# Three loads of x ahead of a store, an add on another engine, and a third float16 first stage in a Fourier-transform kernel

## The chip, the cores and the metric

The kernel runs on one core of a Trainium2 chip. The core has a matrix engine (TensorE, PE in the profile; its weight loads are PEld), three engines for elementwise work (VectorE is DVE, ScalarE is ACT, GpSimd is POOL) and SyncE (SP), which in this kernel issues every transfer. The metric is the device time of one execution in microseconds. The kernel before took 1434.9 us (median of 3 runs, 1434.13 to 1436.1).

## The reference

```python
X = np.fft.rfft(x, axis=1)                  # x is 8 x 3136 x 256, float32
y = np.fft.irfft(X * F[None], n=3136, axis=1)   # F = filt_r + 1j * filt_i
mixed = np.real(np.fft.fft(np.fft.fft(y, axis=1), axis=2))
u = y + mixed
un = (u - mean(u)) / np.sqrt(var(u) + 1e-06)    # over the last axis
out = u + np.maximum(un @ w_ch1, 0.0) @ w_ch2   # w_ch1 256 x 1024, w_ch2 1024 x 256
```

## The kernel before

**What is computed where.** Each of the 8 batches passes through a Fourier transform along the sequence, written as matrix products with tables: `forward1` is the first stage (14 steps of 112 x 512), `forward2` the second stage, the multiplication with the filter and the first stage back, `inverse2` the last stage back, whose results (y, halved into even and odd rows by `store`) go to `dy` in DRAM. Batch 0 works with float32 tables and has a first path of its own: the rows of the first group are formed directly from the tile `near` by the matmuls of L845, without `dy`. What is between the stages goes through DRAM: `bt` to `d_f` (L767, L754 and L760 for `near`), then `d_f` to the pieces `b` (L821).

The second half of the work is cut into 49 groups of 512 rows. For each, y is fetched from `dy` (L968), `prepare` adds the mixed part (matmuls L982, adds L992 on DVE), takes the moments (L1040, L1041), forms the four scales `sb` (L1046 to L1056), the normalised rows `un` (L1151, ACT), their two float16 halves `u` (L1154 on ACT, L1155 on POOL), and transposes them by DMA into `ut` (L1156, on SP). The first group is transposed by PE (L327, `utt`). Then `first_product` (L1181, 6 matmuls for each of 8 slices, followed by L1191 on ACT and L1192 on DVE) and `second_product` (L1211) do the two matrix products of the group. They are most of PE's work. The weights come from float64 words which ACT and DVE widen (L1231 to L1238) and split in halves (L1299, L1312: `w2s` is what L1211 loads).

**The first stage in two forms.** Batches named in `PLAIN`, 1 and 2, multiply x as float32 by a float32 table; the others scale x, split it into float16 halves on ACT and DVE and multiply three times. The step of `forward1`, cut:

```python
            if b in PLAIN:
                nc.tensor.matmul(p, table, x, start=True, stop=True)          # L530
                nc.scalar.activation(st[:, :, 0], p, AF.Copy, scale=sx[:112, 1:2])       # L532
                nc.vector.scalar_tensor_tensor(st[:, :, 1], p, sx[:112, 1:2], st[:, :, 0], ...)  # L533
                ...
            nc.scalar.activation(x16[:, 0], x, AF.Copy, scale=sx[:112, 1:2])  # L538
            nc.vector.scalar_tensor_tensor(x16[:, 1], x, sx[:112, 1:2], x16[:, 0], ...)  # L539
            for i, (hs, hx) in enumerate(((0, 0), (0, 1), (1, 0))):
                nc.tensor.matmul(p, s1[:, hs], x16[:, hx], start=i == 0, stop=i == 2)   # L544
```

L546 and L547 then split the result of the second form. The scale `sx` comes from the squares of x (L480 for batch 1, ahead of need; L319 for others), through a broadcast by PE (L312, `pb_x`).

**What sets the order.** The program calls these pieces from one loop over the slices; `todo`, a list of numbers and functions, says at which step weights and x are loaded and widened. A tile scheduler then puts the instructions of each engine in one order from its own timeline, and each engine runs its order strictly, waiting where an instruction's operands aren't there. `after(...)` forbids that something is put ahead of a named instruction (`"bt", 6`: the last `bt`; `"near"`; `"warm"`: small matmuls on still data, L294, whose results nobody reads; `"utt"`; `"turn"`). SP issues all transfers from one order too, and a transfer waits for the one eight before it.

## Time and profile before

| | |
|---|---|
| median of 3 runs | 1434.9 us (1434.13 to 1436.1) |
| the profiled execution's own time | 1433.79 us |
| its span, first to last instruction | 1432.0 us |
| granted TensorE clock, mean of the span | 0.994 |
| busy: PE, DVE, ACT, POOL | 1387.5, 1042.7, 756.3, 506.7 us |
| instructions | 29958 |

The profiled execution lies 1.1 us under the median. PE is busy 97% of the span; busy shares of the other engines are means over stages with different limits. A wait row says which engine waited at which line and operand for which engine's result; a timeline row gives the start, the length, the engine, the line and the shapes, and in brackets the idle time just before it with what ended it.

### The profile page before, as it was taken

The page shows a single profiled execution, that of the slowest core. Times are in us where ns is not written, and L with a number is a line of the kernel's source. Part 1 is how long each engine was busy: PE and PEld are TensorE (multiplying, and loading weights), DVE is VectorE, ACT ScalarE, POOL GpSimd, SP SyncE. Part 2 cuts the span into 40 slices and gives each one's busy share as a digit, 9 for nine tenths or more (in the row PEclk, how much of TensorE's full clock was granted, in tenths as well). Part 3 has the DMA queues.
Part 4 walks back from the last instruction along what each step waited for, and adds up shares of the span by engine and source line. Part 5 has one row for each costly group of instructions (what it writes and reads, how often), then busy time and mean ns, then how long its engine had stood idle before and what let it go on. Part 6 is the DMA issues. An engine that isn't in the chain of part 4 may idle for free.

```text
span 1432.0 us, 29958 instructions
## 1 busy us (share of the span) xinstructions
PE 1387.5 (97%) x11242; PEld 946.6 (66%) x11242; DVE 1042.7 (73%) x2317; ACT 756.3 (53%) x1421; POOL 506.7 (35%) x643
## 2 busy tenths in 40 slices
PE   8869899999999999999999999999999999999998
PEld 7736576567666776667766676666766667666666
DVE  7867684788698777877588867978779876555553
ACT  6775555546465544746546554655546464434341
POOL 2501681078103930167300960047401762011010
PEclk9989999999999999999999999999999999999999
DMA  9585987699857967579766987589585977452220
GB/s 349 189 272 172 263 201 243 192 224 228 258 155 193 246 160 244 169 204 232 169 224 190 239 193 223 150 242 228 128 272 164 227 177 192 117 154 80 82 59 30
DMA packets 434350, 276.98 MB, mean 193 GB/s; under 512 B 218877, under 2 KB 400845, under 8 KB 434205
## 3 DMA queue, kind: packets, MB, share of 16 engines
q1 hardware_dynamic: 434076, 275.02, 70.0%
q8 instruction: 88, 1.44, 0.4%
q14 instruction: 58, 0.47, 0.1%
q10 hardware_dynamic: 128, 0.05, 0.0%
HBM read 124.87 MB, written 99.17 MB: 156 GB/s over the span
## 4 chain that ended last, share of the span: by engine, by line
PE 70%; DMA 11%; DVE 7%; issue 4%; ACT 3%; POOL 3%; SPq 2%; DVEq 0%; ACTq 0%; POOLq 0%
PE h L1181 27%; PE acc L1211 27%; PE y L880 3%; DMA x<-x 3%; PE s L544 2%; PE mix L982 2%; PE s L530 2%; DMA y<-dy 1%; DMA at<-d 1%; PE i L739 1%; DVE y L992 1%; PE i L741 1%; PE i L740 1%; PE s L640 1%; DVE h L1192 1%
## 5 line engine op out<-in xcount | busy, mean ns | idle before, releaser
L1211 PE MATMUL acc<-w2s,h 128*128 128x256 f16 x4704 | 596.4, 273 | 3.7 <-ACT w2s L1312 2.6
L1181 PE MATMUL h<-ut,home 128*128 128x512 f16 x2352 | 582.0, 380 | 12.4 <-DVE h L1192 7.5
L1211 PEld LDWEIGHTS <-h 128*128 128x128 f16 x4704 | 455.1, 98 | 148.2 <-issue 13.9
L1191 ACT ACTIVATE h<-h 128x512 f16<-128x512 f32 x392 | 232.7, 595 | 375.6 <-PE h L1181 370.1
L1192 DVE SCALAR_TENSOR_TENSOR h<-h,h 128x512 f16<-128x512 f32 x392 | 267.7, 685 | 211.3 <-ACT h L1191 209.4
L1181 PEld LDWEIGHTS <-home 128*128 128x128 f16 x2352 | 221.7, 98 | 223.2 <-issue 33.9
L1155 POOL TENSOR_TENSOR u<-un,u 128x512 f16<-128x512 f32 x96 | 110.4, 1166 | 620.8 <-ACT u L1154 572.3
L992 DVE SCALAR_TENSOR_TENSOR y<-mix,alpha,y 128x508 f32<-128x508 f32 (+1 forms) x360 | 152.9, 476 | 3.9 <-DMA y<-dy 2.0
L657 POOL TENSOR_TENSOR yt<-yt,t 128x224 f32<-128x224 f32 x108 | 73.0, 676 | 130.4 <-DVE t L649 80.7
L1151 ACT ACTIVATE un<-y,sb 128x256 f32<-128x256 f32 x192 | 100.0, 590 | 34.0 <-DVE sb L1056 26.8
L1220 DVE SCALAR_TENSOR_TENSOR y<-acc,beta,y 128x512 f32<-128x512 f32 x98 | 71.3, 744 | 30.3 <-PE acc L1211 30.2
L743 DVE TENSOR_TENSOR bt<-i,bt 112x512 f16<-112x512 f32 x98 | 66.2, 684 | 33.0 <-ACT bt L742 31.2
L687 POOL TENSOR_TENSOR ef<-yt 128x224 f32<-128x224 f32 x112 | 72.2, 663 | 48.7 <-DVE sb L1052 34.8
L889 ACT ACTIVATE ys<-y,alpha 128x512 f32<-128x512 f32 x98 | 64.3, 684 | 40.8 <-PE y L880 40.4
L671 POOL TENSOR_TENSOR home<-yt,home 128x448 f16<-128x448 f32 x77 | 79.3, 1035 | 13.7 <-ACT home L670 13.7
L742 ACT CAST bt<-i 112x512 f16<-112x512 f32 x98 | 56.7, 584 | 45.4 <-PE i L741 41.5
L645 DVE SCALAR_TENSOR_TENSOR yt<-s,pF,ft 128x448 f32<-128x448 f32 x98 | 65.9, 676 | 17.1 <-PE s L641 16.2
L658 POOL TENSOR_TENSOR yt<-yt,t 128x224 f32<-128x224 f32 x108 | 74.6, 693 | 0.6 <-DVE yt L651 0.6
L1040 DVE BATCH_NORM_STATS2 st<-y 128x6 f32<-128x256 f32 x196 | 73.0, 411 | 0.2
L319 DVE TENSOR_REDUCE mx<-x 112x1 f32<-112x1024 f32 x42 | 51.0, 1214 | 23.8 <-DMA x<-x 23.4
L649 DVE SCALAR_TENSOR_TENSOR t<-s,pF,ft 128x448 f32<-128x448 f32 x98 | 66.1, 675 | 0.0
L717 POOL TENSOR_TENSOR eo<-ef,eo 128x448 f16<-128x448 f32 (+6 forms) x55 | 51.5, 940 | 29.3 <-ACT eo L716 27.9
(180 smaller groups left out, 1648.1 us busy)
## 6 DMA issues: line engine op xcount, KB each, us to landing
x<-x SPq DMA_DIRECT2D x55, 512.0 KB
out<-y SPq DMA_DIRECT2D x98, 256.0 KB
at<-d SPq DMA_DIRECT2D x49, 512.0 KB
b<-d SPq DMA_DIRECT2D x49, 512.0 KB
dy<-ys SPq DMA_DIRECT2D x206, 112.0 KB
y<-dy SPq DMA_DIRECT2D x90, 256.0 KB
d<-ast SPq DMA_DIRECT2D x98, 224.0 KB
d<-bt SPq DMA_DIRECT2D x98, 224.0 KB
```

The costliest lines, as they stand in the source:

```text
L657: nc.gpsimd.tensor_tensor(yh[:, 0], yh[:, 0], t2v[:, 1], op=ALU.subtract)
L658: marks["sum"] = nc.gpsimd.tensor_tensor(yh[:, 1], yh[:, 1], t2v[:, 0], op=ALU.add).ins
L671: nc.gpsimd.tensor_tensor(ylo, ytv, yhi, op=ALU.subtract)
L687: nc.gpsimd.tensor_tensor(ef[:, i], yt[:, 0, i], yt[:, 1, i], op=o)
L992: nc.vector.scalar_tensor_tensor(out, p, al, y, op0=ALU.mult, op1=ALU.add)
L1040: nc.vector.bn_stats(st[:m, 2 * t + k], y[:m, t, k])
L1151: nc.scalar.activation(un[:m, k], y[:m, t, k], AF.Identity, bias=sb[:m, i, 1:2], scale=sb[:m, i, 3:4])
L1155: marks["u16", g] = nc.gpsimd.tensor_tensor(u16[:m, :, :, 1], unv, u16[:m, :, :, 0], op=ALU.subtract).ins
L1181: marks["pe"] = nc.tensor.matmul(p[:, c0 : c0 + n].rearrange("p (t k q) -> p t k q", k=2, q=m), homes["w1s"][:, d, hw, 128 * f : 128 * f + ...
L1191: marks["relu"] = nc.scalar.activation(h[:, 0, :nt], p[:, :nt], AF.Relu).ins
L1192: marks["h"] = nc.vector.scalar_tensor_tensor(h[:, 1, :nt], p[:, :nt], 0.0, h[:, 0, :nt], op0=ALU.max, op1=ALU.subtract).ins
L1211: nc.tensor.matmul(acc[:m, k], h[:, hh, c0 : c0 + m], w2s[:, f, hw], start=f == 0 and k == 0 and i == 0, stop=f == 7 and k == 1 and i == 2,)
```

## The change

- `PLAIN` loses batch 2, so its first stage takes the form with halves.
- The first two pieces of batch 0 for `inverse2` are loaded by a new function, `load_piece`, at two numbers of `todo`, after the last `bt`; the mark `"piece"` stands for the last of them. Loads of the weights and the later loads of x now wait for `"piece"` in place of `("bt", 6)`, and x's pieces 5 and 6 for the first `y` piece.
- The first three loads of x move from 57 and 61.2 to 49.1 in `todo`; `take_words` from 56.9 to 49.
- The first pieces of `inverse2` (L903) come after `"turn"` and not after `"warm"`, and the six fillers behind each are gone; 20 fillers stand at one place instead, ahead of the transposes of group 0. `square_x` runs for pieces 0 to 2 together.
- The copy of two columns of `y` in the first group (L1086) moves from ACT to DVE.
- The calls of `give` and `fetch(1)` that stood before the loop move to its step 1, and `give` in the first steps runs at 0, 3 and 5 instead of 1 and 3.

```diff
-PLAIN = (1, 2)
+PLAIN = (1,)
...
-        with after(("bt", 6)):
+        with after("piece", ("y", 1) if q > 4 else ""):
             nc.sync.dma_start(sooner[q], a["x"][1, q])
...
+    pieces = {}
+
+    def load_piece(c):
+
+        bt = fp.tile([128, 4, 256], F32, tag="b2", name=f"b2_0_{c}", bufs=2)
+        with after(("bt", 6)):
+            marks["piece"] = nc.sync.dma_start(bt, blocks128(scratch[2][0], 4 * c, 4)).ins
+        pieces[c] = bt[:112]
+
...
-            if c < 7:
+            if c < 7 and not (b == 0 and c in pieces):
...
-        load(1 if b == 0 else 0)
+        if b:
+            load(0)
...
-                load(c // 2 + 1)
+                if b or c > 2:
+                    load(c // 2 + 1)
...
-            with after("warm" if c < 4 else "turn"):
+            with after("turn"):
                 marks["i2"] = nc.tensor.matmul(
...
-            if c < 4:
-                warm(6, "i2", p=idle[0])
...
-        nc.scalar.copy(y[row, t0, 1, 0:129:128], point[row, 0, 0:129:128])
+        nc.vector.tensor_copy(y[row, t0, 1, 0:129:128], point[row, 0, 0:129:128])
...
-        with after(("bt", 6)):
+        with after("piece"):
             nc.sync.dma_start(words[i], src.bitcast(I32).rearrange("p (n w) -> p n w", w=2))
...
-    todo += [(57, load_x, 0), (57, load_x, 1), (61.2, load_x, 2), (61.5, load_x, 3)]
+    todo += [(56.95, load_piece, 1), (56.96, load_piece, 2)]
+    todo += [(49.1, load_x, 0), (49.1, load_x, 1), (49.1, load_x, 2), (61.5, load_x, 3)]
...
-    todo += [(56.9, take_words, i) for i in (5, 6)]
+    todo += [(49, take_words, i) for i in (5, 6)]
...
-    for q in range(2):
+    for q in range(3):
         square_x(q)
...
-    square_x(2)
     next(first_group)
-    give(come[0] + 2)
+    warm(20, "i2", p=idle[0])
     for _ in first_group:
         pass
+    give(come[0] + 2)
...
-    give(need(511))
-    fetch(1)
...
-        if q in (1, 3) or q > 9:
+        if q in (0, 3, 5) or q > 9:
             give(min(come[0] + 1, soon(32 * q + SOON)))
+        if q == 1:
+            give(need(511))
+            fetch(1)
```

**SP, end of batch 0's first stage back.** Before, the transfers stand in this order, directly behind the loads of `near` (`x_0` to `x_4`: pieces of batch 1's x; `b_0_1`, `b_0_2`: the pieces for `inverse2`; `raw`: words of the weights; `dy`: the first store of y):

```order
L767 DMA d_f<-bt_6_0_763 112x512
L767 DMA d_f<-bt_6_1_772 112x512
L473 DMA x_0_838<-x 128x1024
L473 DMA x_1_840<-x 128x1024
L473 DMA x_2_922<-x 128x1024
L1255 DMA raw_836<-w 128x1024
L821 DMA b_0_1_920<-d_f 128x4x256
L1255 DMA raw_837<-w 128x1024
L473 DMA x_3_926<-x 128x1024
L821 DMA b_0_2_958<-d_f 128x4x256
L473 DMA x_4_1120<-x 128x1024
L826 DMA dy_919<-ys_2_960 28x4x256 x4
```

Now, with `x_0` and `x_1` just ahead of the first row shown (the new code's line 813 is `load_piece`, 1267 the weights):

```order
L473 DMA x_2_744<-x 128x1024
L767 DMA d_f<-bt_5_1_765 112x512
L754 DMA near_282<-d_f 96x1x512
L754 DMA near_283<-d_f 96x1x512
...
L767 DMA d_f<-bt_6_0_771 112x512
L767 DMA d_f<-bt_6_1_780 112x512
L813 DMA b_0_1_844<-d_f 128x4x256
L813 DMA b_0_2_846<-d_f 128x4x256
L1267 DMA raw_722<-w 128x1024
```

The three loads of x have moved ahead of the store of `bt_5_1` and of the loads of `near`; both pieces of `inverse2` have moved ahead of the weights.

**DVE, around the scales of group 2.** Before, the five steps of group 2's `sb` stand in this row, ahead of the adds of group 3's y (L992 of `y_1617`, which come six rows further on):

```order
L1052 RECIPROCAL sb_1535<-sb_1535 128x4
L1041 BN_AGGR mv_1723<-st_1724 128x2
L1053 SCALAR_TENSOR_TENSOR sb_1535<-sb_1535 128x4
L645 SCALAR_TENSOR_TENSOR yt_0_1671<-s_1_0_0_1672,pF,ft 128x448
L649 SCALAR_TENSOR_TENSOR t_1_0_0_1690<-s_1_0_0_1672,pF,ft 128x448
L1054 SCALAR_TENSOR_TENSOR sb_1535<-mv_1533,sb_1535 128x4
L651 TENSOR_TENSOR yt_0_1671<-s_1_0_0_1672,fnyqs 128x1
L1192 SCALAR_TENSOR_TENSOR h_1_5_1718<-h_5_1711,h_1_5_1718 128x512
L1055 SCALAR_TENSOR_TENSOR sb_1535<-sb_1535 128x4
L1056 SCALAR_TENSOR_TENSOR sb_1535<-mv_1533,sb_1535 128x4
```

Now the adds of group 3 (`y_1625`, the new code's line 1004) stand between them:

```order
L1065 SCALAR_TENSOR_TENSOR sb_1543<-sb_1543 128x4
L651 TENSOR_TENSOR yt_0_1679<-s_1_0_1_1762,fnyqs 128x1
L1004 SCALAR_TENSOR_TENSOR y_1625<-mix_1572,alpha_800,y_1625 128x4x127
L1066 SCALAR_TENSOR_TENSOR sb_1543<-mv_1541,sb_1543 128x4
L1204 SCALAR_TENSOR_TENSOR h_1_6_1824<-h_6_1817,h_1_6_1824 128x512
L1004 SCALAR_TENSOR_TENSOR y_1625<-mix_1572,alpha_800,y_1625 128x2x127 x2
L1067 SCALAR_TENSOR_TENSOR sb_1543<-sb_1543 128x4
L1004 SCALAR_TENSOR_TENSOR y_1625<-mix_1572,alpha_800,y_1625 128x4
L691 TENSOR_TENSOR es_1877<-yt_0_1679 128x1
L645 SCALAR_TENSOR_TENSOR yt_1_1790<-s_1_1_0_1791,pF,ft 128x448
L649 SCALAR_TENSOR_TENSOR t_1_1_0_1809<-s_1_1_0_1791,pF,ft 128x448
L1068 SCALAR_TENSOR_TENSOR sb_1543<-mv_1541,sb_1543 128x4
```

The last scale of group 2 has moved behind adds that need a fetch of y from `dy`.

**POOL, the halves of group 2.** Before (`yt`: parts of batch 1's spectrum):

```order
L671 TENSOR_TENSOR home<-yt_0_1671,home 128x4x112
L658 TENSOR_TENSOR yt_0_1671<-yt_0_1671,t_1_0_1_1772 128x224
L1155 TENSOR_TENSOR u_2_0_1553<-un_0_1550,u_2_0_1553 128x4x128
L1155 TENSOR_TENSOR u_2_1_1560<-un_1_1557,u_2_1_1560 128x4x128
L671 TENSOR_TENSOR home<-yt_1_1782,home 128x4x112
```

Now:

```order
L657 TENSOR_TENSOR yt_1_1790<-yt_1_1790,t_1_1_1_1867 128x224
L658 TENSOR_TENSOR yt_1_1790<-yt_1_1790,t_1_1_1_1867 128x224
L700 TENSOR_TENSOR ef_0_1874<-yt_0_1679 1x224
L1167 TENSOR_TENSOR u_2_0_1561<-un_0_1558,u_2_0_1561 128x4x128
L671 TENSOR_TENSOR home<-yt_1_1790,home 128x4x112
L1167 TENSOR_TENSOR u_2_1_1568<-un_1_1565,u_2_1_1568 128x4x128
```

The two halves of group 2 have moved behind both parts of `yt_1`.

## Rows read from the trace of the kernel before

**Rows 1.** The page's head: span, and busy time of each engine
```profile
span 1432.0 us, 29958 instructions
PE 1387.5 (97%) x11242; PEld 946.6 (66%) x11242; DVE 1042.7 (73%) x2317; ACT 756.3 (53%) x1421; POOL 506.7 (35%) x643
```
**Rows 2.** Waits of PE: total us, how many, the longest
```profile
PE y L903 <- DMA b<-d_f: 7.6, 1, 7.6
...
PE h L1181 <- DMA ut<-u: 4.9, 1, 4.9
```
**Rows 3.** Timeline, 66 to 111 us: start, length, engine, line, [idle before, what ended it]
```profile
66.97 1.46 SPq L473 DMA_DIRECT2D x<-x  x3
68.82 1.89 PE L845 MATMUL y<-near,home 120*128 120x256 f32 x8
69.82 0.57 SPq L821 DMA_DIRECT2D b<-d_f  x1
72.63 1.06 ACT L480 ACTIVATE xsq<-x 112x1024 bf16<-112x1024 f32 x1 [5.22 <-DMA x<-x]
73.95 0.69 DVE L1091 TENSOR_TENSOR y<-y,y 128x512 f32<-128x512 f32 x1 [4.33 <-ACT y L1086]
78.29 2.02 PE L903 MATMUL y<-b,i2f 112*112 112x512 f32 x2 [7.58 <-DMA b<-d_f]
78.42 2.08 ACT L1103 ACTIVATE u<-y,sb 128x256 f16<-128x256 f32 x4 [1.05 <-DVE sb L1056]
87.52 2.75 PE L1181 MATMUL h<-ut,home 128*128 128x512 f16 x12
95.29 0.38 SPq L968 DMA_DIRECT2D y<-dy  x1
105.47 0.38 PE L1211 MATMUL acc<-w2s,h 128*128 128x256 f16 x2 [2.61 <-ACT w2s L1312]
110.58 10.43 PE L1211 MATMUL acc<-w2s,h 128*128 128x256 f16 x94
```
**Rows 4.** The chain that ended last, pieces in order of time: start, us, what
```profile
66.50 3.24 DMA d_f<-bt
69.82 8.34 DMA b<-d_f
...
95.72 6.80 DMA x<-x
...
121.01 3.44 PE s L530 x8
...
574.38 1.73 PE s L544 x8
```
**Rows 5.** Timeline, 146 to 166 us, around PE's wait for group 2
```profile
153.32 1.79 DVE L992 SCALAR_TENSOR_TENSOR y<-mix,alpha,y 128x508 f32<-128x508 f32 x4 [1.19 <-DMA y<-dy]
155.16 2.28 POOL L1155 TENSOR_TENSOR u<-un,u 128x512 f16<-128x512 f32 x2
157.87 5.52 SPq L1156 DMA_TRANSPOSE ut<-u  x2
165.50 5.28 PE L1181 MATMUL h<-ut,home 128*128 128x512 f16 x12 [4.86 <-DMA ut<-u]
```
**Rows 6.** Stretches: length, busy PE, PEld, DVE, ACT, POOL, granted clock, DMA share, GB/s
```profile
106.00:110.00 4.00, 3.85 (x6) 1.50 (x6) 4.00 (x17) 2.00 (x5) 0.12 (x1) 0.58 0.43 144
165.00:170.00 5.00, 4.50 (x11) 1.61 (x12) 1.46 (x3) 2.25 (x5) 4.82 (x5) 0.50 0.97 212
260.00:300.00 40.00, 40.00 (x325) 24.44 (x322) 32.68 (x79) 18.95 (x33) 6.81 (x9) 1.00 0.71 212
```
**Rows 7.** Groups by line and form: busy us, mean ns of one, idle before
```profile
L539 DVE SCALAR_TENSOR_TENSOR x<-x,sx,x 112x512 f16<-112x512 f32 x70 | 51.8, 751 | 4.8 <-ACT x L538 4.6
...
L530 PE MATMUL s<-x,s1f 112*112 112x512 f32 x56 | 28.4, 627 | 0.0
```
**Rows 8.** All transposes of `ut` on SP: issue ns min/median/max
```profile
L1156 SPq DMA_TRANSPOSE ut<-u x96: 1231/1258/7486, 115.8 to 1389.9; - x96
```

More of the change, by code (lines that the diff above doesn't have):

```diff
@@ L812, in load @@
         def load(c):
-            if c < 7:
+            if c < 7 and not (b == 0 and c in pieces):
                 shape = [128, 4, 2, 256] if b else [128, 4, 256]
                 bt = fp.tile(shape, F16 if b else F32, tag="b2", name=f"b2_{b}_{c}", bufs=2)
-                bts[c] = bt[:112]
                 with after("dy"):
@@ L822, in load @@
                     marks["b", c] = marks["sp"] = move.ins
+                (bts if b else pieces)[c] = bt[:112]
+        if b == 0:
+            bts = pieces
         def store(k, s, r, ys, c, j0):
```

## The prediction

> **What bounds the kernel now.** I read the head of the page first [rows 1]: PE is busy for 1387.5 of 1432.0 us, 97%, and DVE, the next, for 1042.7. So PE bounds the whole, and a change can pay in two ways only: it takes work from PE, or it fills some of the 44.5 us in which PE waits. The waits of PE come next [rows 2], since they tell where these us are. Two that the change can touch are a single wait of 7.6 us of L903 for a piece of `d_f` and one of 4.9 us of L1181 for the transposes. Then the timeline says where they lie, at 78.29 and 165.50 us, and shows a third in its bracket, 2.61 us of L1211 for the weights at 105.47 [rows 3, 5]. Last, the granted clock of the stretch behind such a wait: 0.58 from 106 to 110 us and 0.50 from 165 to 170 [rows 6], the lower of the two levels, 1.2 GHz, against 1.00 in a full stretch such as 260 to 300. A wait of PE thus costs more than its own length: 0.42 of 4 us, 1.7, behind the first, 2.5 of 5 us behind the second.
>
> Everything below is summed against the profiled execution, 1433.8 us, which lies 1.1 under the median of the runs; 1.1 is added at the end.
>
> **Part 1, the start of the groups (66 to 111 us).** Before, the direct sums end at 68.82 + 1.89 = 70.7 us, but the first add of group 0 (L1091) comes at 73.95 [rows 3]. Its bracket names the copy L1086 on ACT, and the row above names what held ACT: the squares L480, which waited 5.22 us for x, whose three loads were issued from 66.97 on. The change takes this away twice over: the copy goes to DVE, and the loads of x are issued ahead of the loads of `near`, so that no square waits for them. The add then follows the sums directly: 73.95 - 70.7 = 3.2 us earlier. L903 no longer stands between the sums and PE's transposes of group 0. The halves of `u` that PE transposes were done at 78.42 + 2.08 = 80.5, and L1181 came at 87.52, 7.0 us on [rows 3]. In these PE did the second half of L903's row, 12 fillers, two more L903 matmuls, and only then the transposes, whose results are copied to `ut`. The copies and transposes I estimate at half of the 7.0, so some 3.7 us go with L903 behind the transposes and fillers that wait for nothing. So L1181 could start 6.9 us earlier than 87.52, at 80.6.
>
> Against it stands a delay d: the three loads of x, 1.5 MB, now stand on SP ahead of the store of `bt_5_1`, and the loads of `near` for the direct sums need this store. No row shows such a store behind three loads, so I bound it. The lower end is near nothing, 0.3 us for three more issues (1.46 us for three at 66.97 [rows 3], mostly in SP's idle time); less than nothing is excluded, since no transfer that the store needs goes earlier. The upper end is from the piece `b`, which landed 8.34 us after its issue behind the same three loads, where the `bt` store ahead of it took 3.24 [rows 4]: 5.1 us. I take 1.6, nearer the lower end, since at 57 us fewer other transfers are under way than at 70. L1181 then starts at 82.2, 5.3 us earlier.
>
> The Trainium skill, page "DMA: Bandwidth & Descriptors", section "Two DMAs through the same engine are not ordered", says that descriptors of one queue of a DMA engine start in their order. This speaks against the change: the store would begin only behind the loads, and d would be near the upper end, with a part 1 smaller by some 2 us than the sum has it. The row of `b` fits it only partly, since its 8.34 us held some transfers issued ahead of the loads as well.
>
> Not all 5.3 us reach the second products. L1211 waits until 105.47 for `w2s` on ACT [rows 3], which stands there behind the square of x's last piece. This piece is a transfer of 6.80 us from 95.72, landing at 102.5 [rows 4], right behind the fetch of y issued at 95.29 [rows 3]. This fetch moves up by some 3.5 us only, since ahead of it `dy` must be stored from the L903 pieces that now come later. With it the piece of x lands 3 to 3.5 us earlier, and L1211 starts at about 102.5. Compared at equal work: before, from 105.47 to 110.58, PE did 5.1 us at a lowered clock, or some 2.7 us of work at the full one; that point corresponds to 107.9 for a full clock without a loss. Now it is 102.5 plus about 2.2 for the same lowered stretch, 104.9. **Gain 3.0 us**, between 0.5 (d at its upper end) and 5.3 (all of L1181's start).
>
> **Part 2, group 2 (146 to 166 us).** Count from S, the end of the first block of batch 1's spectrum on PE, 146.6 us. Before, PE reached group 2's first product at S + 14.0 (160.6) and the transposes landed at S + 18.9 (165.5) [rows 5]. The order after puts matmuls of `i`, `s` and half a `mix` ahead of that product, about 3.0 us of work that stood behind it. So the landing that loses nothing is S + 21.9.
>
> The chain to it is longer now. The last scale of group 2 stands behind group 3's adds, which wait for a fetch of y: before, the adds began at 153.32 = S + 6.7 [rows 5]. The rows from the adds to the last scale are some 5 us by the durations of their like (the adds alone 1.79 for four), so S + 11.8. Then `un` on ACT, about 2; the casts, about 1.2; POOL, which must finish `yt_1` first; two halves of `u` at 2.28 / 2 each with a `home` of 1 between them: S + 19. From the end of POOL's `u`, 157.44, to the landing at 165.5 were 8 us, of which SP's two transposes, 5.52, were the most [rows 5]; the median transpose is 1.258 [rows 8], so 3 to 6 us here. The landing is between S + 22 and S + 25; I take S + 22.9, nearer the short end, because the transposes are issued apart and not one behind the other. **Loss 1.0 us**, between 3.5 and, should the fetch or POOL come much earlier, a gain of up to 7.4 (the wait of 4.9 and the 2.5 of the low clock).
>
> **Part 3, batch 2's first stage.** Before, a float32 step stands as two rows of PE: the 28 steps of the two batches are 56 rows of L530 [rows 7]. Eight such rows take 3.44 us in the chain, 0.43 each, and eight of the float16 matmuls 1.73, 0.216 each [rows 4]. So a step is 2 x 0.43 = 0.86 us before and 3 x 0.216 = 0.65 after, 0.21 less: 14 x 0.21 = 2.9 us of PE. DVE gets 14 x 0.751 = 10.5 us more (L539) [rows 7], ACT about as much. In the stretch where this lies DVE is busy for 32.68 of 40 us, ACT for 18.95 [rows 6], so there is room for some 7 of DVE's 10.5 in the stretch and for the rest beside later work. The relu of L1192 stands in the same row of DVE, and where DVE fills up PE waits for it; I take 1.0 us lost to this. **Gain 1.9 us**, between 0.5 and 2.9.
>
> The rest (names taken earlier, `give` at other steps, L903 without fillers later on) moves work between places where PE is busy all the time; I cost it at nothing, with PE's own queue of work as the cover, full over whole stretches (40.00 of 40 from 260 to 300 us [rows 6]), and 1 us either way where that cover is gone.
>
> **The sum**: 3.0 - 1.0 + 1.9 = 3.9 us. 1433.8 - 3.9 = 1429.9, with 1.1 for the median **1431.0 us**. All three parts at their likely ends give 1428 to 1434.
>
> **The rivals.**
> *A, group 2's wait goes altogether.* With 3.0 us more work ahead of it and a fetch that comes with part 1's lead, the transposes land in time. For it: the row of 5.52 us on SP was long against a median of 1.258, and needn't repeat. Against it: the scales now stand behind the adds. It gives 8.4 us over the forecast's part 2: about 1423.
> *B, the x loads hold the store.* d is 5 us or more, L1181 starts hardly 2 us earlier, part 1 falls to about 1. For it: the 8.34 us of `b`. Against it: other transfers were ahead of `b` too. About 1433.
> *C, slower: group 2's transposes come late.* The place is SP and POOL at S + 17 to S + 30. The two transposes of group 2 have another transpose between them, and one can take 7.486 us on SP [rows 8]. Landing at S + 30 costs 30 - 21.9 = 8.1 instead of 1.0: 1438. It decides from a landing at S + 26.8 on, where the loss, 4.9, has eaten parts 1 and 3. For it: four engines stand in this chain, each in strict order. Against it: the median transpose.
> *D, batch 2 gives back its gain.* DVE fills to 40 of 40 and PE waits for L1192 or L539: part 3 is nothing or below, about 1433. For it: 32.68 + 10.5 is over 40. Against it: another batch's matmuls of this form run without a gap, eight in 1.73 us [rows 4].
>
> **How the numbers follow.** 0.2% is 2.9 us, about what a measurement of this kernel tells from no change: faster is below 1432.0, slower above 1437.8. Forecast 0.50, A 0.13, B 0.17, C 0.12, D 0.08. The forecast's own range, 1428 to 1434, is faster for four fifths. Faster: 0.40 + 0.13 + 0.03 from B's better end = 0.56. Slower: 0.11 from C and 0.02 from D. Same: 0.31. The range of 8 in 10 reaches from 1424, leaving out half of A and more, to 1437, leaving out C's late landings.
>
> **What would show it.** Part 1: the add of group 0 directly behind the direct sums, L1181 starting near 82, L1211 near 102.5; a start of the direct sums more than 3 us later than before would be B. Part 2: PE's wait for `ut` of group 2, 4.9 us before, of 5 to 7 us by the forecast, none by A, over 10 by C. Part 3: the float16 form's matmuls 42 more, and PE's waits for DVE's L1192, with DVE's busy time up by some 10 us. I would be wrong above all if the waits after 300 us, which I left alone, move by more than 2 us.

## The result and the profile after

The changed kernel takes 1453.3 us (median of 4 runs, 1448.57 to 1460.27) against 1435.5 for the kernel before in the same job (4 runs, 1434.13 to 1441.28). The ratio is 1.0131, with an interval of 1.0106 to 1.0157: 1.3% slower, where 0.3% faster was forecast, and far outside the range. The profiled execution took 1453.24 us.

The head of the page after, to be held against [rows 1]:

```profile
span 1451.5 us, 30030 instructions
...
PE 1393.9 (96%) x11264; PEld 950.7 (66%) x11264; DVE 1055.1 (73%) x2332; ACT 762.6 (53%) x1434; POOL 506.5 (35%) x643
```

PE idles 1451.5 - 1393.9 = 57.6 us, before 44.5: 13.1 more. Its busy time went up by 6.4 although the change takes work from it; the granted clock, below, can say why. The two forms of the first stage in the list of groups (busy us, mean ns of one):

```profile
L544 PE MATMUL s<-x,s 112*112 112x512 f16 x252 | 72.1, 380 | 0.0
...
L530 PE MATMUL s<-x,s1f 112*112 112x512 f32 x28 | 13.3, 592 | 0.0
```

L530 lost 28.4 - 13.3 = 15.1 us [rows 7] and L544 gained 72.1 - 59.8 = 12.3 (210 of these took 59.8 us before), so PE was spared 2.8 us, about the 2.9 that were forecast. That gain is there and is buried. The waits of PE after (total us, times, longest), against [rows 2]:

```profile
PE i L739 <- DMA z<-y: 8.5, 4, 3.0
PE h L1193 <- DVE h L1204: 7.5, 7, 2.4
PE acc L1223 <- ACT w2s L1324: 7.2, 1, 7.2
PE y L857 <- DMA near<-bt: 5.2, 1, 5.2
PE s L640 <- DMA at<-d: 4.2, 5, 1.5
PE i L739 <- DMA z<-home: 4.1, 3, 1.9
...
PE h L1193 <- DMA ut<-u: 1.8, 2, 0.9
```

Line numbers are 12 higher here from `load_piece` on: L857 is L845 of before, L1193 is L1181, L1204 is L1192, L1223 is L1211, L1324 is L1312. The waits for L903 (7.6) and for group 2's transposes (4.9) have gone. In their place stand waits that were shorter or absent: `near` (none before), `w2s` (2.6 us before), and many short ones for the transposed tiles `z` (3.8 before) and for `at` (1.9). The waits for the relu on DVE are as long in all as they were:

```profile
PE h L1181 <- DVE h L1192: 7.5, 8, 2.1
```

The start in the timeline after (start, length, engine, line, idle before with what ended it), against [rows 3]:

```profile
59.68 0.35 SPq L767 DMA_DIRECT2D d_f<-bt  x1
67.23 1.41 SPq L754 DMA_DIRECT2D near<-d_f  x2
...
72.65 3.48 PE L857 MATMUL y<-near,direct 120*128 120x256 f32 x8 [5.16 <-DMA near<-bt]
75.97 1.89 PE L857 MATMUL y<-near,home 120*128 120x256 f32 x8
...
86.93 2.76 PE L1193 MATMUL h<-ut,home 128*128 128x512 f16 x12
...
98.19 0.51 SPq L473 DMA_DIRECT2D x<-x  x1
99.21 0.43 SPq L473 DMA_DIRECT2D x<-x  x1
...
104.39 1.06 ACT L480 ACTIVATE xsq<-x 112x1024 bf16<-112x1024 f32 x1 [4.18 <-DMA x<-x]
...
108.15 0.59 PE L1223 MATMUL acc<-w2s,h 128*128 128x256 f16 x2 [7.23 <-ACT w2s L1324]
```

The store of `bt_5_1` is issued at 59.68 behind the three loads of x, and the loads of `near`, which wait for it, at 67.23. Before, they were issued at 61.35:

```profile
61.35 1.42 SPq L754 DMA_DIRECT2D near<-d_f  x2
```

So d is 67.23 - 61.35 = 5.9 us. Some 1.5 of it is the store's own later issue (58.14 before), the other 4.3 its longer way to the dependent loads. PE waits 5.16 us for `near`, takes 3.48 us for the next eight sums (1.89 for the eight after them), and ends the sums at 77.9 instead of 70.7.

Four stretches of the two kernels (length, busy PE, PEld, DVE, ACT, POOL, then granted clock, DMA share, GB/s), before:

```profile
60.00:110.00 50.00, 36.62 (x175) 19.00 (x174) 36.53 (x102) 32.78 (x67) 6.84 (x12) 0.90 0.70 235
140.00:220.00 80.00, 73.88 (x698) 52.76 (x697) 65.12 (x146) 40.98 (x80) 57.47 (x76) 0.96 0.90 218
220.00:350.00 130.00, 125.38 (x1054) 81.62 (x1053) 90.34 (x211) 73.50 (x139) 55.29 (x73) 1.00 0.84 227
350.00:650.00 300.00, 296.13 (x2466) 201.48 (x2463) 235.54 (x519) 163.49 (x305) 109.59 (x137) 1.00 0.75 205
```

and after, with one short stretch more behind the wait for `w2s`:

```profile
60.00:110.00 50.00, 35.55 (x184) 19.65 (x183) 35.80 (x93) 32.01 (x64) 6.69 (x11) 0.90 0.70 231
140.00:220.00 80.00, 71.57 (x677) 50.97 (x675) 60.94 (x133) 38.84 (x76) 54.45 (x72) 0.94 0.87 212
220.00:350.00 130.00, 121.70 (x1017) 79.81 (x1016) 93.97 (x208) 76.59 (x144) 45.24 (x59) 0.99 0.78 216
350.00:650.00 300.00, 291.00 (x2385) 195.70 (x2383) 236.39 (x520) 160.84 (x301) 105.91 (x133) 0.99 0.76 199
...
103.00:113.00 10.00, 4.65 (x22) 3.05 (x22) 7.33 (x26) 6.08 (x12) 1.28 (x2) 0.50 0.78 270
```

Length less PE's busy time is PE's idle time: 13.4, 6.1, 4.6 and 3.9 us before; 14.5, 8.4, 8.3 and 9.0 after. The start does not win but loses 1.1, and the idle time grows by 2.3 at group 2's place, by 3.7 where batch 2's first stage lies, and by 5.1 from 350 to 650, which I had not looked at. In the ten microseconds from 103 on, the end of the wait for `w2s` and what follows it, the granted clock is 0.50, the 1.2 GHz level, and the mean of the whole span is 0.989 after 0.994 before. Matmuls at the lower level count as busy for longer, which is where the 6.4 us of busy time can come from.

### The profile page after: what moved, and what is told of

Read it like the earlier page. It is cut to its first block, busy times and chain, and to the rows that moved or that the text cites. A ratio compares the mean times of both kernels' runs of the same rounds, so it can differ in the third digit from the quotient of the medians.

```text
span 1451.5 us, 30030 instructions
## 1 busy us (share of the span) xinstructions
PE 1393.9 (96%) x11264; PEld 950.7 (66%) x11264; DVE 1055.1 (73%) x2332; ACT 762.6 (53%) x1434; POOL 506.5 (35%) x643
## 4 chain that ended last, share of the span: by engine, by line
PE 64%; DMA 11%; DVE 8%; issue 5%; ACT 4%; POOL 4%; SPq 3%; DVEq 0%; ACTq 0%; POOLq 0%
PE h L1193 25%; PE acc L1223 24%; DMA x<-x 4%; PE s L544 3%; PE y L894 2%; PE mix L994 2%; DMA at<-d 2%; DVE y L1004 2%; ACT un L1163 1%; DVE h L1204 1%; DMA z<-y 1%; PE i L739 1%; SPq L838 1%; PE i L741 1%; PE i L740 1%
## 5 line engine op out<-in xcount | busy, mean ns | idle before, releaser
L1223 PE MATMUL acc<-w2s,h 128*128 128x256 f16 x4704 | 600.8, 274 | 11.7 <-ACT w2s L1324 7.2
L1193 PE MATMUL h<-ut,home 128*128 128x512 f16 x2352 | 583.4, 382 | 9.8 <-DVE h L1204 7.5
L1223 PEld LDWEIGHTS <-h 128*128 128x128 f16 x4704 | 456.1, 98 | 159.7 <-issue 15.3
L1204 DVE SCALAR_TENSOR_TENSOR h<-h,h 128x512 f16<-128x512 f32 x392 | 267.7, 684 | 215.9 <-ACT h L1203 214.2
L1193 PEld LDWEIGHTS <-home 128*128 128x128 f16 x2352 | 222.3, 98 | 220.5 <-issue 32.3
L1167 POOL TENSOR_TENSOR u<-un,u 128x512 f16<-128x512 f32 x96 | 110.4, 1165 | 624.7 <-ACT u L1166 617.7
L657 POOL TENSOR_TENSOR yt<-yt,t 128x224 f32<-128x224 f32 x108 | 72.7, 673 | 140.6 <-DVE t L649 93.2
L687 POOL TENSOR_TENSOR ef<-yt 128x224 f32<-128x224 f32 x112 | 71.9, 661 | 50.5 <-DVE eo L722 49.0
L903 ACT ACTIVATE ys<-y,alpha 128x512 f32<-128x512 f32 x98 | 63.9, 684 | 42.7 <-PE y L894 42.3
L671 POOL TENSOR_TENSOR home<-yt,home 128x448 f16<-128x448 f32 x77 | 79.1, 1031 | 19.8 <-ACT home L670 19.7
L658 POOL TENSOR_TENSOR yt<-yt,t 128x224 f32<-128x224 f32 x108 | 74.4, 691 | 0.0
L544 PE MATMUL s<-x,s 112*112 112x512 f16 x252 | 72.1, 380 | 0.0
L739 PE MATMUL i<-z,i 112*112 112x256 f16 x196 | 54.9, 280 | 12.8 <-DMA z<-y 8.5
```

The source lines that it names most:

```text
L657: nc.gpsimd.tensor_tensor(yh[:, 0], yh[:, 0], t2v[:, 1], op=ALU.subtract)
L658: marks["sum"] = nc.gpsimd.tensor_tensor(yh[:, 1], yh[:, 1], t2v[:, 0], op=ALU.add).ins
L671: nc.gpsimd.tensor_tensor(ylo, ytv, yhi, op=ALU.subtract)
L1167: marks["u16", g] = nc.gpsimd.tensor_tensor(u16[:m, :, :, 1], unv, u16[:m, :, :, 0], op=ALU.subtract).ins
L1193: marks["pe"] = nc.tensor.matmul(p[:, c0 : c0 + n].rearrange("p (t k q) -> p t k q", k=2, q=m), homes["w1s"][:, d, hw, 128 * f : 128 * f + ...
L1204: marks["h"] = nc.vector.scalar_tensor_tensor(h[:, 1, :nt], p[:, :nt], 0.0, h[:, 0, :nt], op0=ALU.max, op1=ALU.subtract).ins
```

## The experiments

All ratios are to the runs of the kernel before on the same chip in the same job, whose medians were 1435.3 to 1437.8 us.

### The two parts apart

**e1_before_halves**: the halves alone, in the kernel before.

```diff
-PLAIN = (1, 2)
+PLAIN = (1,)
```

> The kernel before with one edit: batch 2's first stage from float16 halves; its start is untouched up to some 240 us. Theory H (the halves cost more than they give: DVE's 10.5 us more in the stretch of batch 2 make PE wait): 8 to 12 us slower than before, about 1445, with PE's waits between 300 and 420 us up by 5 or more, as in the changed kernel (30.2 us of PE's idle time up to 330 us before, 36.7 after). Theory S (the start alone is guilty, the halves give what was forecast): 1 to 3 us faster, about 1432.5.

Measured: 1444.7 us, ratio 1.0062 (1.0038 to 1.0087), 8.9 us slower, as theory H had it. PE's idle time from 300 to 420 us is 7.3 us, 2.2 before.

**e2_after_plain**: the new start alone, that is, the changed kernel with batch 2 in float32 again.

```diff
-PLAIN = (1,)
+PLAIN = (1, 2)
```

> The changed kernel with batch 2's first stage from float32 x again, so the new start alone. Theory H: what is left is the loss up to 300 us, 5 us at equal work of PE, so 1439 to 1441. Theory S: 15 to 18 us slower than before, about 1451.

Measured: 1446.9 us, 1.0081 (1.0055 to 1.0107), 11 us slower, between the ranges of the two theories. Each part loses by itself, and 0.62 + 0.81 = 1.43% is, within the intervals, the 1.31% of both. So no meeting of the two parts is needed to explain the result; each has to be explained alone.

### The start: the loads of x ahead of the store

**e4_plain_x_late**: as e2, but the loads of x stand behind the pieces, and their squares where the weights are split.

```diff
-    todo += [(49.1, load_x, 0), (49.1, load_x, 1), (49.1, load_x, 2), (61.5, load_x, 3)]
+    todo += [(57, load_x, 0), (57, load_x, 1), (57, load_x, 2), (61.5, load_x, 3)]
...
-    for q in range(3):
-        square_x(q)
...
     give(come[0] + 2)
+    for q in range(3):
+        square_x(q)
```

> As the run with the new start alone, but the three loads of x stand behind the pieces of y (numbers 57), and their squares behind group 0. Theory L (the store of bt_5_1 lands late because three loads of x stand ahead of it): the loads of near are issued at 61 to 62 us instead of 67.2, group 0's first product starts at 81 to 83 instead of 86.9; the time falls by 2 to 6 us against the new start alone. Rival M (the store is late for another reason): near stays at 67, no change of the start.

**e5_x_at_46**: as e2, but the loads of x stand earlier still, ahead of more of the `bt` stores.

```diff
-    todo += [(49.1, load_x, 0), (49.1, load_x, 1), (49.1, load_x, 2), (61.5, load_x, 3)]
+    todo += [(46, load_x, 0), (46, load_x, 1), (46, load_x, 2), (61.5, load_x, 3)]
```

> As the run with the new start alone, but the three loads of x are issued earlier still, behind bt_2_1 and ahead of bt_3_0 (number 46). Theory L: by the time of bt_5_1's store the loads have landed, near is issued at 61 to 62 us, group 0's first product starts at 81 to 83 us; 2 to 6 us faster than the new start alone. Rival M: near stays near 67. If instead the stores of bt_3 and bt_4 are late by 5 us and PE's matmuls of near's first half with them, the cost has only moved.

Measured: e4 1441.2 us, 1.0037 (1.0018 to 1.0056); e5 1442.1 us, 1.0050 (1.0031 to 1.0069). With e2 at 1446.9, moving the loads out of the store's way, to either side, gives back 5 to 6 us by the medians. The timeline of e4:

```profile
58.13 0.30 SPq L767 DMA_DIRECT2D d_f<-bt  x1
61.36 1.42 SPq L754 DMA_DIRECT2D near<-d_f  x2
...
81.49 2.76 PE L1193 MATMUL h<-ut,home 128*128 128x512 f16 x12
...
98.62 0.38 PE L1223 MATMUL acc<-w2s,h 128*128 128x256 f16 x2 [1.67 <-ACT w2s L1324]
```

From the store's issue to the loads that wait for it are 3.2 us here and 7.5 in the changed kernel, and in e5 the loads of `near` go out at 61.26: the cause of d is shown from both sides. L1193 starts 6.0 us sooner than before and L1223 6.9 sooner (98.62 against 105.47). Not all of the 6.9 is the store's doing, since e4 also moves the squares of x, and `w2s` now stands ahead of the last of them on ACT. In e5, where the squares stand as in the changed kernel, L1193 starts at 82.11 and L1223 at 102.45, 3.0 sooner than before. So in both the start does what it was meant to do, and yet e4 is 0.37% slower than before and e5 0.50%. e4's first two stretches show where its lead goes:

```profile
60.00:110.00 50.00, 42.02 (x249) 25.43 (x248) 40.56 (x110) 35.73 (x72) 9.42 (x15) 0.97 0.74 245
140.00:220.00 80.00, 68.73 (x666) 49.18 (x664) 60.56 (x132) 39.84 (x78) 58.43 (x77) 0.98 0.89 208
```

PE idles 8.0 us instead of 13.4 in the first, and 11.3 instead of 6.1 in the second: what was won is lost again by 220 us. (The profiled execution, 1436.4, lies 5 us under e4's median, so the profile shows less than the whole loss.)

### Where the lead goes, 140 to 220 us

From 140 to 350 us, e4's PE waits for `z` and ACT where it waited for `ut` before:

```profile
PE i L739 <- DMA z<-y: 6.3, 3, 3.7
PE acc L1223 <- ACT h L1203: 3.1, 4, 1.3
PE i L739 <- DMA z<-home: 2.4, 2, 1.8
```

The transposes `z` are fed by the halves of batch 1's spectrum, whose low half POOL forms (L671), in the same queue as group 2's `u` (L1167). Three suspects: POOL has too much to do; the DMA engines are full; or the order in POOL's and DVE's queues is wrong.

**e6_low_on_dve** (POOL gets less: one of batch 1's low halves on DVE) and **e7_fold_twice** (POOL gets more: batch 1's sums of L687 are done twice, the second time for nothing, 9.2 us). Both on top of e4.

```diff
-            nc.gpsimd.tensor_tensor(ylo, ytv, yhi, op=ALU.subtract)
+            low = nc.vector if b == 1 and hf else nc.gpsimd
+            low.tensor_tensor(ylo, ytv, yhi, op=ALU.subtract)
```

> The new start with x's loads behind the pieces (the best of the four runs so far, 1441.2), and of batch 1's spectrum seven of the 14 subtractions L671 go from POOL (1.03 us each) to DVE. Theory P (the lead of 13 us that this start has at 157 us is lost up to 215 us because the parts of batch 1's spectrum come from POOL at POOL's pace, 17 of 20 us busy): PE's waits for z (L739, 1.8, 3.7, 0.8 and 0.6 us between 157 and 217) shrink by 3 us or more, 1437 to 1439. Rival D (DVE sets the pace, or the order of the work does): the waits stay or grow, 1441 to 1444.

```diff
-                    nc.gpsimd.tensor_tensor(ef[:, i], yt[:, 0, i], yt[:, 1, i], op=o)
+                    for _ in range(2 if b == 1 else 1):
+                        nc.gpsimd.tensor_tensor(ef[:, i], yt[:, 0, i], yt[:, 1, i], op=o)
```

> The same start, with POOL's sums L687 for batch 1 (14 of 0.66 us) done twice, so 9.2 us more of POOL in the stretch from 150 to 215 us and nothing else; the result is the same. Theory P: PE's waits for z grow by nearly all of it, 6 to 9 us slower than without, about 1448. Rival D: POOL has the room, 0 to 2 us, about 1442.

Measured: e6 1442.6 us, 1.0039 (1.0028 to 1.0051), no better than e4; e7 1443.6, 1.0048 (1.0031 to 1.0065), some 2 us worse than e4 by the ratios, for 9.2 us of extra work. Both intervals overlap e4's, so POOL's load is hardly it. e6 alone would not show this, since it gives DVE what it takes from POOL.

**e10_tables_sooner** (the pieces of the float16 stages' tables are loaded two at a step and so earlier, and fewer transfers fall between 140 and 200 us) and **e11_tables_twice** (each piece of `c_i` loaded twice, 1.6 MB more there), both on top of e4.

```diff
             next(halves, None)
+        if q > 5:
+            next(halves, None)
```

> The new start with x's loads behind the pieces (1441.2, ratio 1.0037, as run before), and the tables of the float16 stages (seven pieces of c_i, 224 KB each) are loaded two at a step, so ahead of 140 us and not up to 166. Theory Q (the lead of that start is lost between 140 and 190 us because the DMA engines are full there, share 1.03 against 0.63 from 120 to 140 us, so that fetches of y, transposes of ut and z land at DMA's pace): 1.1 MB less in that stretch at 240 GB/s is 4.6 us; PE reaches 207 us's work 2 to 4 us sooner and the time falls by as much, to 1437 to 1439, ratio 1.001 to 1.002. Rival C (the chain of four engines in strict order sets the pace, DMA's share only goes with it): no change, ratio 1.003 to 1.005.

```diff
-                nc.sync.dma_start(i1_rows[:, 4 * ch : 4 * ch + 4], a["c_i1"][:, 4 * ch : 4 * ch + 4])
+                for _ in range(2):
+                    nc.sync.dma_start(i1_rows[:, 4 * ch : 4 * ch + 4], a["c_i1"][:, 4 * ch : 4 * ch + 4])
```

> The same start, with each piece of c_i loaded twice into its place: 1.6 MB more, most of it between 140 and 170 us; nothing else changes. Theory Q: PE's waits between 145 and 210 us grow by 4 to 7 us, ratio 1.006 to 1.009. Rival C: under 2 us, ratio 1.003 to 1.005.

Measured: e10 1439.0 us, 1.0019 (0.9995 to 1.0044); e11 1443.6 us, 1.0060 (1.0042 to 1.0078). Less and more traffic go the way the theory says, but each interval overlaps that of e4. A part at most. The waits of e10 say why it is not more. From 140 to 220 us, PE's waits for `z` fall from e4's 6.8 us to 0.9, and in their place PE waits for group 2's transposes, for which it does not wait in e4:

```profile
PE h L1193 <- DMA ut<-u: 5.9, 1, 5.9
```

**e14_before_sooner**: e10's edit in the kernel before.

```diff
             next(halves, None)
+        if q > 5:
+            next(halves, None)
```

> The kernel before with the seven pieces of c_i loaded two at a step, so ahead of 140 us and not beside the fetch and transposes of group 2 (DMA share 0.87 from 140 to 160 us, 1.07 from 160 to 180). Theory Q (DMA's fullness makes the transposes of group 2 late): PE's wait of 4.9 us for them shrinks to 1 to 3 us, and with it the slow clock; ratio 0.996 to 0.998. Rival C (the chain of scale, un, u and SP's order sets it): wait of 4 to 6 us as before, ratio 0.999 to 1.003.

Measured: 1437.1 us, 1.0013 (0.9999 to 1.0027). Earlier tables bring nothing to the kernel before, where the wait for `ut` stays (5.3 us).

**e15_before_pe_twice** and **e16_new_pe_twice**: is the lead lost because PE now runs ahead of the chain and waits for it? Then more work on PE at that place should cost nothing. The first half of group 1's first products is done twice: 24 matmuls at 0.216 us as in [rows 4], 5.2 us; e15 in the kernel before, e16 in e4.

```diff
-        for ts, c0, n, m in runs:
+        for ts, c0, n, m in runs * (2 if g == 1 and f < 4 else 1):
```

> The kernel before, in which four of the eight slices of group 1's first product are done twice: 24 matmuls of 0.216 us, 5.2 us more of PE between 125 and 150 us; the result is the same. Theory E (behind the start PE's pace doesn't count up to some 207 us: it waits there for group 2's transposes, 4.9 us, and the work is hidden in that wait): ratio 0.999 to 1.002. Rival F (PE's lead or lag at 150 us is kept to the end): ratio 1.003 to 1.004.

> The same addition behind the new start with x's loads behind the pieces of y (ratio 1.0037 without it). Theory E (its lead is slack ahead of the chains of batch 1's spectrum): ratio 1.003 to 1.005, PE's waits for z between 157 and 217 us (7.4 us in sum) down by 3 to 5. Rival F: ratio 1.007 to 1.008.

Measured: e15 1446.1 us, 1.0077 (1.0055 to 1.0099): 11 us slower for 5.2 us of work. e16 1432.4 us, 0.9972 (0.9958 to 0.9986): with 5.2 us more work it is 9 us faster than e4, and faster than the kernel before. Both are outside either theory's range, and the amount of work can't be the reason for opposite signs. The scheduler had rewritten the order of the other engines as well. On POOL, group 2's first half of `u` stands behind three sums of batch 1's spectrum (L657, L658) in e16, behind eight in e4; it starts at 156.0 us in both. But in e15 it stands behind two, behind six in the kernel before, and e15 is slower. So the place of `u` alone does not decide. Against the kernels that they start from, PE's idle time falls by 9.4 us in e16 and grows by 3.0 in e15.

**e17_new_pe_half**: as e16, with half as much put in.

```diff
-        for ts, c0, n, m in runs:
+        for ts, c0, n, m in runs * (2 if g == 1 and f < 2 else 1):
```

> The same start, two slices of group 1's first product done twice (2.6 us of PE, half of e16), in an order in which u of group 2 stands behind both parts of yt_1. Theory R: ratio 1.002 to 1.006, as without the work. Rival G (more work of PE ahead of group 2 is itself what helps): ratio 0.999 to 1.001, between the two.

Measured: 1439.0 us, 1.0019 (1.0003 to 1.0035). POOL's `u` is again behind eight of batch 1's sums here, as in e4, and the time is between those of e4 and e16. It fits the order as the cause, but also an effect that grows with the work, so it separates less than I had hoped.

**e20_scales_first**: e4 with the order changed and no work added. The adds of group 3 may not stand ahead of group 2's `un`, so that the scales of group 2 no longer stand behind them.

```diff
-            with after(("u16", 0), "wide", ("lines", "w2")) if g == 1 else after("h", *((("un", 1), "w2l") if g == 2 else ())):
+            with after(("u16", 0), "wide", ("lines", "w2")) if g == 1 else after("h", *((("un", 1), "w2l") if g == 2 else (("un", 2),) if g == 3 else ())):
```

> The new start with x's loads behind the pieces of y (ratio 1.0037), with one mark more: group 3's adds may not be put ahead of group 2's scales. The scales then stand together ahead of the adds, and u of group 2 on POOL ahead of all of batch 1's spectrum. Theory R (the order at group 2 loses the start's lead): ratio 0.996 to 0.999, PE's waits between 157 and 217 us down by 3 us or more. Rival G (it is the amount of work or the run's own scatter): ratio 1.002 to 1.005.

**e21_scales_first_sooner**: the same edit on top of e10.

> The mark of e20 and the tables of c_i two at a step. Theory R with DMA's share (1.03 from 140 to 180 us) as a second cause: ratio 0.994 to 0.998, a little below e20. If the tables are no cause: as e20.

Measured: e20 1439.1 us, 1.0015 (1.0003 to 1.0027); e21 1432.3 us (1428.75 to 1439.37), 0.9975 (0.9957 to 0.9993). Group 2's first `u` on POOL in the timeline of e4, then of e20:

```profile
156.05 1.15 POOL L1167 TENSOR_TENSOR u<-un,u 128x512 f16<-128x512 f32 x1
```

```profile
146.29 1.17 POOL L1167 TENSOR_TENSOR u<-un,u 128x512 f16<-128x512 f32 x1
```

The mark does move `u` ahead, by 10 us, but e20's time lies between the ranges of theory R and rival G. From 140 to 220 us its PE idles 6.4 us, e4's 11.3, so at its own place the order gives back what was forecast of it:

```profile
140.00:220.00 80.00, 73.58 (x700) 52.69 (x699) 64.05 (x149) 41.26 (x81) 58.41 (x77) 0.98 0.89 220
```

Behind that, in this one execution, PE idles 6.2 us from 220 to 350 and 6.7 from 350 to 650 (e4: 5.9 and 4.6). The order alone (e20) and the tables alone (e10) each bring 2 to 3 us over e4, with overlapping intervals. Together they bring 9: e21's interval lies clear of those of e20 and e4, and just clear of e10's. The waits fit this. From 140 to 220 us e10, with the tables alone, is rid of the waits for `z` and has the one for `ut` (0.9 and 5.9 us); e20, with the order alone, has no wait of note for `ut` but those for `z` (0.2 and 5.1); e21 has 1.9 us for `z` and none for `ut`. The first two stretches of e21:

```profile
60.00:110.00 50.00, 43.06 (x245) 25.98 (x244) 39.12 (x106) 35.09 (x71) 10.11 (x16) 0.93 0.75 253
140.00:220.00 80.00, 75.57 (x722) 54.86 (x721) 62.96 (x142) 44.11 (x87) 61.01 (x79) 0.98 0.82 200
```

PE idles 6.9 and 4.4 us: the lead of the start is kept past 220 us. e21 is 0.25% faster than the kernel before. It gets there with three things: the new start without x ahead of the store, the order of group 2, and the earlier tables. It does not use the halves.

### The halves

**e9_dead_halves**, **e12_dead_dve**, **e13_dead_act**: the kernel before with float32 matmuls as they were, to which the two elementwise steps per x piece are added, unread: 14 of each, DVE's alone, ACT's alone.

```diff
             if b in PLAIN:
+                if b == 2:
+                    x16 = fp.tile([112, 2, 2, 256], F16, tag="x16", name=f"x16_{b}_{q}", bufs=3)
+                    nc.scalar.activation(x16[:, 0], x, AF.Copy, scale=sx[:112, 1:2])
+                    nc.vector.scalar_tensor_tensor(
+                        x16[:, 1], x, sx[:112, 1:2], x16[:, 0], op0=ALU.mult, op1=ALU.subtract
+                    )
```

(In e12 the line of `nc.scalar` is left out and the last operand is `x`; in e13 the three lines of `nc.vector` are left out.)

> The kernel before with float32 matmuls in batch 2, to which the 14 steps L538 on ACT and 14 L539 on DVE are added, whose results nobody reads: the halves' cost on ACT and DVE without their matmuls and without PE waiting for them. Theory V: the load itself slows, 8 to 12 us slower than before, about 1446. Rival O: PE waits for none of it, 0 to 3 us, about 1437.

> The kernel before with 14 steps of L539's size on DVE alone in batch 2's first stage, whose results nobody reads (no L538 on ACT): 10.5 us of DVE. The pair of both cost 7.3 us (ratio 1.0051). Theory V1 (it is DVE's load): ratio 1.004 to 1.006. Theory V2 (it is ACT's, whose casts make the u of a group late): ratio 0.999 to 1.002.

> The same with the 14 steps L538 on ACT alone, 10.1 us of ACT and nothing on DVE. Theory V1: ratio 0.999 to 1.002. Theory V2: ratio 1.004 to 1.006.

Measured: e9 1444.3 us, 1.0051 (1.0024 to 1.0077); e12 1441.5, 1.0039 (1.0017 to 1.0060); e13 1438.2, 1.0010 (0.9993 to 1.0027). The load on DVE alone costs 6 us and ACT's hardly anything that can be told from none; the sum is that of the pair. The load alone thus costs most of the 8.9 us of e1, and PE's 2.8 us do not make up for it. What waits for it is not chiefly the first stage itself. Between 140 and 350 us, PE waits more for the transposes `ut` of the groups, first in e12, where L1186 is L1181, then in e1. The longest of each list, 4.7 us, is the wait for group 2 that the kernel before has too (4.9), ahead of the added steps; the other two are new:

```profile
PE h L1186 <- DMA ut<-u: 8.3, 3, 4.7
```

```profile
PE h L1181 <- DMA ut<-u: 7.3, 3, 4.7
...
PE s L544 <- ACT x L538: 0.7, 1, 0.7
```

Only 0.7 us in that list is L544's wait for its own operand on ACT. The 14 steps stand in DVE's queue ahead of adds, moments and scales of the next group, and these come late. The rows of the kernel before, from DVE's last step on the scale of x to the last scale of that group and to the issue of its transposes:

```profile
253.19 0.15 DVE L316 TENSOR_SCALAR sx<-sx 128x1 int32<-128x1 int32 x1
...
271.88 0.16 DVE L1056 SCALAR_TENSOR_TENSOR sb<-mv,sb 128x4 f32<-128x4 f32 x1
...
276.63 1.25 SPq L1156 DMA_TRANSPOSE ut<-u  x1
```

The same in e12, and PE's wait behind it, where the kernel before has none:

```profile
250.35 0.15 DVE L316 TENSOR_SCALAR sx<-sx 128x1 int32<-128x1 int32 x1
...
279.34 0.16 DVE L1061 SCALAR_TENSOR_TENSOR sb<-mv,sb 128x4 f32<-128x4 f32 x1
...
284.07 1.25 SPq L1161 DMA_TRANSPOSE ut<-u  x1
...
289.36 4.12 PE L1186 MATMUL h<-ut,home 128*128 128x512 f16 x12 [2.60 <-DMA ut<-u]
```

From the scale of x to the group's last scale it is 18.7 us before and 29.0 in e12: 10.3 more, as long as the 14 steps take. The granted clock from 280 to 300 us is 0.91 in e12, 1.00 before. How much of e12's 6 us is this delay, and how much the other changes of order that the scheduler makes after the edit, is not separated.

**e8_halves_pool**: e1 with the low half of batch 2 on POOL, in two steps, since POOL has the most idle time (35% busy).

```diff
+            if b == 2:
+                nc.gpsimd.tensor_scalar(x, x, sx[:112, 1:2], None, op0=ALU.mult)
+                nc.gpsimd.tensor_tensor(x16[:, 1], x, x16[:, 0], op=ALU.subtract)
+            else:
```

> The kernel before with batch 2's first stage from float16 halves (1444.7 as run before), but the low half made by POOL (a scaling of x in place and a subtraction) and not by DVE. POOL is idle from 240 to 260 us and hardly busy up to 300. Theory V (the halves cost 9 us because DVE gets 10.5 us more work in a stretch where its queue has no room): the loss goes, 1431 to 1437. Rival O (the price is not DVE's load: the chain scale, ACT, low half, matmul is longer than the one of float32, and the order that the scheduler makes is another): 1441 to 1448, above the kernel before by 6 or more, since POOL's two steps are longer still.

Measured: 1467.1 us, 1.0206 (1.0183 to 1.0229), 29 us slower and far above both ranges. The two groups of instructions that POOL gained, and PE's longest wait between 140 and 350 us (L644 is L640):

```profile
L540 POOL TENSOR_SCALAR x<-x,sx 112x512 f32<-112x512 f32 x14 | 21.8, 1565 | 38.6 <-ACT x L538 38.6
L541 POOL TENSOR_TENSOR x<-x,x 112x512 f16<-112x512 f32 x14 | 15.9, 1156 | 0.2
```

```profile
PE s L644 <- DMA at<-d: 9.4, 1, 9.4
```

A step takes 1.565 + 1.156 = 2.7 us on POOL, 0.75 on DVE [rows 7]. Now the first stage itself comes late, and with it the transposed tile `at` that the second stage reads. The engine with the most idle time was the worse place of the two.

## Why the prediction was wrong

**What bounds the kernel** was read rightly: waits of PE make the difference, and the clock is lower behind them (0.50 from 103 to 113 us after). Too few of them were looked at. The prediction took up those that the change was meant to take away, and counted the rest at nothing.

**Part 1, the term d failed.** The order of steps was right. Counted from the end of the direct sums to the first L1193, before took 87.52 - 70.71 = 16.8 us and after 86.93 - 77.86 = 9.1: 7.7 us saved, where 6.9 were forecast. But d was taken as 1.6 us "nearer the lower end" and measured 5.9, beyond the upper end of 5.1; with the slow sums behind the wait, the sums end 7.15 us later. So L1193 starts at 86.9 and not at 82.2. That is rival B's mechanism, at more than its price: the store's later issue alone, 1.5 us, is nearly all of the d that I took. The row of `b`, 8.34 us [rows 4], was the nearest there was, and I argued it away with a guess about other transfers. The rule of the Trainium skill (page "DMA: Bandwidth & Descriptors", section "Two DMAs through the same engine are not ordered") that descriptors of one queue start in order spoke for the upper end, and the trace agrees: 7.5 us from store to dependent load behind the loads of x, 3.2 without them (e4), with all of SP's transfers in one queue of the profile.

**Part 1, the second products** came late with it. L1223 was to start at 102.5 and started at 108.15. The landing of x that holds `w2s` was rightly named, but its last two loads were issued at 98.19 and 99.21, where the last one before went out at 95.72 [rows 4]: the diff puts them behind the fetch of y (`("y", 1)`). I had that fetch move up by 3.5 us; it came at 97.19, 1.9 us later than before, since the start was late. In e5, without d, it came at 91.23, 4.1 earlier than before, and L1193 (82.1) and L1223 (102.45) started where the sum has them (82.2 and 102.5). So d is the one step of part 1 that failed. And a right part 1 would not have been enough: e5 has it, without the halves, and is 0.50% slower than the kernel before.

**Part 2** looked at one wait of several. The wait for group 2's `ut` was to be 5 to 7 us and is gone, which is rival A's sign but not its gain of 8.4. PE came late to it, because at the same place it first waited for `z` (6.3 us from 140 to 220 after, 1.3 before); there it idles 8.4 us after and 11.3 in e4, 6.1 before. Where the waits for `z` are gone (e10), the one for `ut` is 5.9, within the forecast. So the chain to `ut` was read rightly, and the failed step is that no other chain was priced. "Four engines stand in this chain, each in strict order" is what I wrote for rival C; other chains, that to `z` first of all, go through the same queues.

**Part 3**: the 2.9 us of PE came true (2.8). The loss, taken as 1.0 us, was about 12 in e1 (8.9 slower although PE is spared 2.8: 11.7). The failed step is "there is room for some 7 of DVE's 10.5 in the stretch". DVE was busy 32.68 of 40 us [rows 6], but an idle slot in a queue that runs strictly in order is not room: the new steps stand ahead of work for which PE waits. e12 shows it without any change to PE's work: its 14 unread steps put the next group's last scale 10.3 us further from the scale of x, and the kernel takes 6 us longer. Rival D had the direction and saw too small a price, since it let only L1192 and L539 come late.

**"The rest ... at nothing"** had a full PE queue as its cover. The prediction said that it would be wrong above all if waits after 300 us moved by more than 2 us. They did: from 350 to 650 us PE idles 5.1 us more, in waits for `h` on DVE (4.1 us, before 2.1), `at` (2.4, before 0.8) and `z` (2.4, before 0.6). e1 has the same 5 us more with the halves alone:

```profile
350.00:650.00 300.00, 291.11 (x2407) 196.81 (x2405) 233.83 (x507) 161.12 (x300) 107.61 (x135) 1.00 0.76 202
```

Whether it is the halves' own doing is not shown: e2, without them, idles 1.5 us more there than the kernel before, but e7, also without them, 4.4 more.

**The range** was too narrow for a reason that the sum had no term for. The scheduler makes the orders anew after an edit. One that adds 5.2 us of work moved the time by +11 in one kernel (e15) and by -9 in another (e16), so by +6 and -14 beyond the work itself. How much of that the order alone does is not shown: e20, which changes nothing but an order, moved e4 by 2 to 3 us.

**Two sums of the prediction** are slightly off by their own terms: 102.5 plus 2.2 is 104.7 and not 104.9, so part 1's gain would be 3.2 us and not 3.0, and a landing at S + 25 is 3.1 us behind S + 21.9 and not 3.5. Neither bears on the outcome.

**What stays open**: how the 0.37% of e4 divides between the order of group 2 and the DMA traffic, as e10 and e20 each lie too near to e4, and only both together are clear; that each covers the other's wait is read from one execution of each. Whether e16 is faster by its order alone was not isolated; e17 doesn't exclude an effect of the work itself. Where the 5 us from 350 to 650 us come from, where batch 3 has the halves in all kernels, I can't name: the waits are many and short. Of e1's 11.7 us, some 7 are the dead load's (e9); the rest is not accounted for. And single profiles carry some 5 us: e4's ten runs went from 1433.89 to 1444.98.

## What to carry to other kernels

Loads moved ahead of a small store in one queue hold up everything that waits for that store, here by some 6 us for 1.5 MB, so look for what stands behind before moving a load up. An engine's busy share does not tell whether it can take more work: ask what stands behind the new step in its queue, and try the step as dead work in the old kernel before building on it. When a wait is taken away and the time doesn't move, compare PE's idle time stretch by stretch: the lead may be lost 50 us later to another chain through the same queues, and a change of order there can give it back.

## What the runs showed of the hardware that I had not expected

- A store of one 112 x 512 tile issued behind 1.5 MB of loads held its dependent load's issue for 7.5 us, against 3.2 us in e4 without the loads. From 57 to 65 us the DMA engines are busy at a share of 0.82 to 0.99 in each microsecond; the dependent load goes out at 67.23.
- A DMA transpose of `z` from `y` took 2.73 us at 161.72 in e4's chain and another of the same form 6.75 at 182.33; the rows don't say what it met.
- POOL needs 1565 ns for a scaling of 112 x 512 float32 values and 1156 ns for the subtraction to float16; DVE does both in one step of 751 ns.
